# Attention and experts in one kernel: the first maxima in two-bank tiles, and the row maxima of later pairs one slot later

## The chip, the cores and the metric

One core of a Trainium2 chip runs the program once. The metric is the device time of that execution in microseconds, the median of several runs. TensorE (PE) has a granted clock that the profile shows; its two levels are 1.2 and 2.4 GHz, and 1.00 is the upper one.

## The reference

Attention over 8 batches of 8 heads, 1152 keys of 64 numbers, queries pooled by two (576), followed by a layer of 8 experts, of which each token uses one.

```python
    q_pool = q.reshape(B, H, S // factor, factor, D).mean(axis=3)
    scores = scale * np.matmul(q_pool, k.transpose(0, 1, 3, 2))
    scores = scores - np.max(scores, axis=-1, keepdims=True)
    attn = np.exp(scores)
    attn = attn / (np.sum(attn, axis=-1, keepdims=True) + 1e-09)
    return np.matmul(attn, v).astype(np.float32)
    ...
        h = np.maximum(x[mask] @ w1[e], 0.0)
        out[mask] = gate_w[mask, None] * (h @ w2[e])
```

## The kernel before

Two heads make a pair; 32 pairs, counted from 0, go through attention one behind the other, and 18 blocks of tokens go through the experts behind them. Numbers of 32 bits are split into a high and a low half of 16 bits (`hi`/`lo`, `qh`, `VH`/`vl`, `Pe`/`Pl`), so that TensorE works on 16-bit operands.

A pair takes three passes. The **maximum pass** (`maxpass`, L952) multiplies rounded queries `QB` with rounded keys `hi`, in tiles of 512 keys, for nine groups of 128 queries (L964), and VectorE reduces each tile to one maximum per query (`mp`, L965). The last 128 keys of four groups share one tile (L972, L973), and the last group has one of its own. At the end VectorE reduces the maxima of all tiles to `m` (L925), TensorE transposes `m` into a row (L929), VectorE scales it (`mr`, L938), and a DMA on SP's queue puts the row below the queries in `B2` (L939), where the score matmuls subtract it. The **scores** (L1031, L1032) are computed in tiles of 432 columns, ScalarE takes the exponential (`Pe`, L1033), and ScalarE and VectorE make its low half (`Pl`, L1014, L1016). The **products** with the values (L1090 to L1092) add up in `xp`, which VectorE scales (L1108 to L1113) and splits (`x`, L1059).

The order of all engines is written out by the program itself: `attention` counts steps, 18 to a pair, and a string of letters per step says when the score generator (`s`), the product generator (`v`) and the maximum generator (`M`, and at some steps `X`) advance by one tile. Tables such as `T_MAX` say at which step, counted from the pair's own first score, the maximum pass of a pair joins the queue; `T_MX2` and `T_MX3` do so for pairs 2 and 3. When a pass has advanced past its last tile, `m` is issued at once and the transpose at the end of that step. The queues of the engines are in order: what stands behind a waiting instruction waits too.

The start differs. The first pair's queries and keys come in pieces (`load_kq`). VectorE adds the two halves of the pooled queries (L1189), ScalarE copies them into `QB` (L1191, L1194) and rounds the keys to `hi` (`split_hi`, L794), GpSimd makes the low halves (`split_lo`, L810). `first_max` (L981) computes the maxima of the first five groups in 15 tiles of 384 keys, one PSUM bank and one reduction each (L988), with a dummy matmul (`busy`) behind every tile, which keeps TensorE's clock up. Then follow the row of these five groups, `T_PRE` tiles of the rest of the pass with two dummies before each, and the first step. SP's queue meanwhile issues the placements of `hi`, `qh` and `lo` into the score operands `B1` and `B2`, for the first head and a part of the second, and then the row. GpSimd fills the last row of both `B2` with a constant (L1180). `alone` marks a VectorE instruction that uses the port of SBUF which it shares with GpSimd, `behind` lets a GpSimd instruction wait for the last one so marked.

Of the kernel before, what the change touches and what calls it, by code (L numbers as in the profile page):

```python
# [9 lines left out]
F32 = mybir.dt.float32  # L10
# [6 lines left out]
ALU = mybir.AluOpType  # L17
AX = mybir.AxisListType
PSUM = bass.MemoryType.PSUM
# [3 lines left out]
P = 128  # L23
# [5 lines left out]
S = 1152  # L29
D = 64  # L30
# [7 lines left out]
ROW = 16.0  # L38
# [29 lines left out]
T_QH = (-26, -32)  # L68
T_HI = (-29, -24)
T_LO = ((-26, -26, -23), (-23, -26, -23))  # L70
T_MAX = -24
T_PLACE = -17
T_REST = -13
ST = 2
# [68 lines left out]
DONE = object()  # L143
ORD = ('NvJMvsvMsvXF', 'JvvsMvvXFvv', 'vFvvsJvXv')
FIRST = (0, 1)
T_PRE = 3
TWO_ROWS = (1,)
X_ALL = 8
X_SOME = 105
X_IN = 3  # L150
T_MX2 = -23
T_MX3 = -23
FIN = 0
FD = 0
PD = 0
# [8 lines left out]
def drain(g):  # L164
    for _ in g:
        pass
# [528 lines left out]
def attention(tc, ctx, att, ident, npairs, xpool, on_two, on_split, on_scale, jobs, side, set_pm, started, ahead, hip, own_port):  # L695
# [3 lines left out]
    nc = tc.nc  # L699
# [2 lines left out]
    const = ctx.enter_context(tc.tile_pool(name="acon", bufs=1))  # L702
    pvl = ctx.enter_context(tc.tile_pool(name="avl", bufs=3))
    sm = ctx.enter_context(tc.tile_pool(name="asm", bufs=3))
    ps_max = ctx.enter_context(tc.tile_pool(name="psmax", bufs=3, space=PSUM))
    ps_sc = ctx.enter_context(tc.tile_pool(name="pssc", bufs=3, space=PSUM))
    ps_pv = ctx.enter_context(tc.tile_pool(name="pspv", bufs=2, space=PSUM))
    small = lambda: ps_pv.tile([P, 512], F32, name="pj", tag="pv")
    some = lambda i: ps_max.tile([P, 512], F32, name="pm") if i in IN_PM else small()
    set_pm(some)  # L710
# [2 lines left out]
    B2, QB, VH, VS = [], [], [], []  # L713
# [8 lines left out]
    st = {p: {} for p in range(npairs)}  # L722
    made = set()
# [59 lines left out]
    def place_qb(p):  # L783
        qh = st[p]["qh"]
        for j in range(2):
            r = slice(j * D, (j + 1) * D)
            move(QB[p % 2].rearrange("p u n -> p (u n)")[r, j * SQ:(j + 1) * SQ], qh[r])

    def split_hi(p, i):
        s = st[p]  # L790
        made.add((p, f"hi{i}"))
        n = 2 if p > 1 else 3
        r = slice(i * S // n, (i + 1) * S // n)
        nc.scalar.copy(s["hi"][:, r], s["k"][:, r])  # L794

    def split_lo(p, i):

        s = st[p]
        made.add((p, f"lo{i}"))
        if p > 1:  # L800
            need(p, ("qh", "hi0", "hi1")[i])
        n = 1 if p > 1 else 3
        if i < n:
            r = slice(i * SQ // n, (i + 1) * SQ // n)
            o, t, h = s["lo"][:, S:KQ], s["q"], s["qh"]
        else:
            w = 576 if n == 1 else 288
            r = slice((i - n) * w, (i - n + 1) * w)
            o, t, h = s["lo"], s["k"], s["hi"]
        x = nc.gpsimd.tensor_tensor(o[:, r], t[:, r], h[:, r], op=ALU.subtract)  # L810
        if p > 2:
            behind(x)

    kcol = lambda j: slice(j * S, (j + 1) * S)
# [18 lines left out]
    def place_q(p, heads):  # L833

        s = st[p]
        for b in (B2[p % 2], s["B1"]):
            for j in heads:
                move(b[0:D, qcol(j)], s["qh"][half[j]])
# [8 lines left out]
    def place_lo(p, heads, k):  # L847

        s = st[p]
        for j in heads:  # L850
            if k:
                move(B2[p % 2][0:D, kcol(j)], s["lo"][half[j], 0:S])
            else:
                move(s["B1"][D:P, qcol(j)], s["lo"][half[j], S:KQ])
# [126 lines left out]
    def first_max(p):  # L981

        s = st[p]
        mp = s["mp"] = sm.tile([P, 9, 3], F32, name="mp")
        for i, (u, t) in enumerate([(u, t) for us, ts in (((0, 1), (0, 1)), ((2, 3), (0, 1)), (range(4), (2,)), ((4,), range(3))) for t in ts for u in us]):
            pt = ps_sc.tile([P, 512], F32, name="psc") if i % 2 else ps_max.tile([P, 512], F32, name="pm")
            nc.tensor.matmul(pt[:, 0:384], QB[p % 2][:, u], s["hi"][:, t * 384:(t + 1) * 384], start=True, stop=True)
            nc.vector.tensor_reduce(mp[:, u, t:t + 1], pt[:, 0:384], op=ALU.max, axis=AX.X)  # L988
            busy(1, 256)
            yield  # L990
        busy(4)
        row(p, mp, 0, 5)()
# [179 lines left out]
    def busy(n, w=512):  # L1172
        for _ in range(n):
            nc.tensor.matmul(idle[:, 0:w], zero[:, 0:P], zero[:, 0:w], start=True, stop=True, skip_group_check=True)

    busy(7)
    for i in range(2):
        nc.vector.memset(QB[i], 0.0)
    for i in range(2):
        nc.gpsimd.memset(B2[i][D:D + 1, 0:2 * S], ROW)  # L1180
    split_q(0)
    q0, qb = st[0]["q"][:, 0:SQ], QB[0].rearrange("p u n -> p (u n)")
    if npairs > 1:
# [2 lines left out]
    for n, i in ((0, 0), (2, 1), (2, 2)):  # L1186
        if i < 2:
            both = st[0]["q"].rearrange("p (w n) -> p w n", w=2)
            nc.vector.tensor_tensor(both[:, 0, half_q(i)], both[:, 0, half_q(i)], both[:, 1, half_q(i)], op=ALU.add)  # L1189
        if i == 0:  # L1190
            nc.scalar.copy(qb[0:D, half_q(0)], q0[0:D, half_q(0)])  # L1191
        split_hi(0, i)
        if i == 1:
            nc.scalar.copy(qb[0:D, half_q(1)], q0[0:D, half_q(1)])  # L1194
        for _ in range(2):
            next(first)
    nc.scalar.copy(st[0]["qh"], q0)
    nc.scalar.copy(qb[D:P, SQ:S], q0[D:P])
    for i in (3, 4, 5, 6, 0, 1, 2):
# [3 lines left out]
    place_q(0, (0,))  # L1203
    place_lo(0, (0,), 1)
    place_lo(0, (0,), 0)
    place_q(0, (1,))
    place_lo(0, (1,), 0)
    if npairs > 1:
        split_q(1)
        for i in range(3):  # L1210
# [10 lines left out]
        for i in (3, 4, 5, 6):  # L1221
            split_lo(1, i)
    drain(first)
    mp0 = st[0]["mp"]
    if npairs > 1:
        place_qb(1)
    place_lo(0, (1,), 1)
    place_k(0, (1,))
    power(0)
# [548 lines left out]
```

## Time and profile before

| what | value |
|---|---|
| median of 3 runs | 1113.68 us (1113.42 to 1114.29) |
| the profiled execution | 1112.91 us |
| its span | 1110.9 us |
| busy: PE, DVE, ACT, POOL | 1096.5, 956.1, 897.0, 428.6 us |
| first scores of pair 0 | 16.66 us after the span's start |

The span runs from the first to the last instruction of the profiled execution. Engines: PE is TensorE (PEld its weight loads), DVE VectorE, ACT ScalarE, POOL GpSimd, SP SyncE, which here issues DMAs. A matmul's line lasts from its start to its modelled end and overlaps with the next, so the distance between starts is what a matmul costs. A bracket behind a line gives the idle time of that engine before it and what ended it.

### The profile page before, as it was taken

What the parts mean: (1) busy time and instruction counts of PE and PEld (TensorE: products, weight loads), DVE (VectorE), ACT (ScalarE), POOL (GpSimd) and SP (SyncE); (2) the same over time, 40 slices, a digit from 0 to 9 for tenths busy, and PEclk for the clock granted to TensorE, in tenths of its full rate; (3) what the DMA queues carried; (4) which work ended last, traced back from release to release, by engine and by line L of the source; (5) the groups of instructions that cost most, each with busy time, mean ns of one, the idle gap of its engine ahead of it and who ended that gap; (6) DMA issues with size and microseconds to landing.
All of it is one profiled execution on the core that took longest, in us unless ns stands there. A gap on an engine that the chain in (4) does not pass through costs nothing. (4 is left out here: it accounts for less than half of the span.)

```text
span 1110.9 us, 36821 instructions
## 1 busy us (share of the span) xinstructions
PE 1096.5 (99%) x15104; PEld 811.7 (73%) x15104; DVE 956.1 (86%) x1960; ACT 897.0 (81%) x1444; POOL 428.6 (39%) x426
## 2 busy tenths in 40 slices
PE   7999999999999999999999999999999999999997
PEld 4777777777777777777777777876677677667675
DVE  8999999999999999999999999789987666756751
ACT  6899999999999999999999999876556566656651
POOL 9765434454444354444534453132122231121111
PEclk9999999999999999999999999999999999999999
DMA  8758756758676667576676755699889999999980
GB/s 253 185 166 200 182 156 177 196 152 198 157 201 175 168 184 191 143 185 180 181 179 165 205 132 127 178 294 312 278 258 239 301 307 290 271 275 287 271 194 33
DMA packets 173248, 228.46 MB, mean 206 GB/s; under 512 B 91039, under 2 KB 125503, under 8 KB 173072
## 3 DMA queue, kind: packets, MB, share of 16 engines
q1 hardware_dynamic: 166944, 206.25, 68.0%
q0 software_dynamic: 6128, 19.79, 6.5%
q8 instruction: 120, 1.97, 0.7%
q14 instruction: 56, 0.46, 0.2%
HBM read 141.92 MB, written 18.99 MB: 145 GB/s over the span
## 5 line engine op out<-in xcount | busy, mean ns | idle before, releaser
L1033 ACT ACTIVATE Pe<-psc 128x432 int32<-128x432 f32 x768 | 375.5, 526 | 35.6 <-PE psc L1032 27.1
L965 DVE TENSOR_REDUCE mp<-pm 128x1 f32<-128x512 f32 x566 | 372.9, 684 | 11.7 <-PE pm L964 4.4
L1090 PE MATMUL xp<-VH,Pe 128*128 128x65 f16 x2880 | 372.8, 193 | 0.0
L1092 PE MATMUL xp<-VS,Pl 128*128 128x65 f16 x2880 | 372.1, 193 | 0.0
L1091 PE MATMUL xp<-vl,Pe 128*128 128x64 f16 x2880 | 370.9, 192 | 0.0
L1091 PEld LDWEIGHTS <-Pe 128*128 128x128 f16 x2880 | 267.6, 98 | 88.0
L1031 PE MATMUL psc<-B 128*128 128x432 f16 (+2 forms) x1152 | 304.1, 286 | 0.9 <-ACT Pe L1033 0.9
L1032 PE MATMUL psc<-B 65*128 65x432 f16 (+2 forms) x1152 | 304.8, 287 | 0.0
L1090 PEld LDWEIGHTS <-Pe 128*128 128x128 f16 x2880 | 271.9, 98 | 39.8 <-issue 1.7
L1092 PEld LDWEIGHTS <-Pl 128*128 128x128 f16 x2880 | 266.5, 97 | 0.0
L1014 ACT ACTIVATE Pl<-Pe 128x1152 f16<-128x1152 uint16 x186 | 216.5, 1164 | 5.9
L964 PE MATMUL pm<-hi,QB 128*128 128x512 f16 x566 | 213.8, 379 | 1.1 <-DVE mp L965 1.0
L1459 PE MATMUL ph<-xpart,w1l 128*128 128x256 f16 x544 | 148.3, 273 | 0.0
L1458 PE MATMUL ph<-xpart,w1h 128*128 128x256 f16 x544 | 148.3, 273 | 0.0
L1457 PE MATMUL ph<-xpart,w1h 128*128 128x256 f16 x544 | 148.3, 273 | 0.0
L810 POOL TENSOR_TENSOR lo<-rawk,hi 128x576 f16<-128x576 f32 (+1 forms) x68 | 83.3, 1228 | 152.8 <-DVE Pl L1016 131.4
L908 POOL TENSOR_SCALAR VH<-rawv,sc 128x512 f16<-128x512 f32 (+1 forms) x63 | 108.5, 1723 | 76.4 <-PE xp L1092 34.5
L1032 PEld LDWEIGHTS <-B 65*128 65x128 f16 x1152 | 112.9, 98 | 24.1 <-issue 1.1
L1031 PEld LDWEIGHTS <-B 128*128 128x128 f16 x1152 | 112.5, 98 | 5.6 <-issue 0.3
L1548 PE MATMUL po<-w2h,hl 128*128 128x512 f16 x288 | 109.1, 379 | 0.0
L1547 PE MATMUL po<-w2l,hh 128*128 128x512 f16 x288 | 109.1, 379 | 0.0
L1546 PE MATMUL po<-w2h,hh 128*128 128x512 f16 x288 | 109.1, 379 | 0.0
(304 smaller groups left out, 1767.9 us busy)
## 6 DMA issues: line engine op xcount, KB each, us to landing
w2r<-in_w_dram SPq DMA_DIRECT2D x72, 512.0 KB
w1r<-in_w_dram SPq DMA_DIRECT2D x68, 512.0 KB
rawv<-in_att_dram SPq DMA_DIRECT2D x32, 576.0 KB
B<-hi SPq DMA_DIRECT2D x128, 144.0 KB
rawq<-in_att_dram SPq DMA_DIRECT2D x31, 576.0 KB
rawk<-in_att_dram SPq DMA_DIRECT2D x31, 576.0 KB
B<-qh SPq DMA_DIRECT2D x128, 72.0 KB
B<-lo SPq DMA_DIRECT2D x64, 144.0 KB
```

Of the source, the lines that this page charges most:

```text
L964: nc.tensor.matmul(pm, QB[p % 2][:, u], s["hi"][:, t * 512:(t + 1) * 512], start=True, stop=True)
L965: nc.vector.tensor_reduce(mp[:, u, t:t + 1], pm, op=ALU.max, axis=AX.X)
L1014: nc.scalar.activation(low, rest, AF.Copy, scale=LOW)
L1031: nc.tensor.matmul(o, b1[:, ks], b1[:, qs], start=True, stop=False, skip_group_check=True)
L1032: nc.tensor.matmul(o, b2[:, ks], b2[:, qs], start=False, stop=True, skip_group_check=True)
L1033: nc.scalar.activation(Pe[:, D + x0:D + x1], pt, AF.Exp, scale=1.0 / 16)
L1090: nc.tensor.matmul(out, Ph[:, qs], vh[:, c, j, 0:D + 1], start=c == 0 and g == 0, stop=False, skip_group_check=True)
L1091: nc.tensor.matmul(out[:, 0:D], Ph[:, qs], vl[:, c, j], start=False, stop=False, skip_group_check=True)
L1092: nc.tensor.matmul(out, Pl[:, qs], vs[:, c, j, 0:D + 1], start=False, stop=c == NKC - 1, skip_group_check=True)
L1457: nc.tensor.matmul(o, hi[:, c, fs], xh[:, :, c], start=c == 0, stop=False)
L1458: nc.tensor.matmul(o, hi[:, c, fs], xl[:, :, c], start=False, stop=False)
L1459: nc.tensor.matmul(o, lo[:, c, fs], xh[:, :, c], start=False, stop=c == 3)
```

## The change

`first_max` takes tiles of two banks: two maxima tiles of 384 keys are computed into one PSUM tile and reduced by one instruction, eight reductions in place of 15. The pool of these tiles is closed before the pools of the maximum and score tiles are opened. VectorE instead of ScalarE rounds the first third of the keys, and VectorE instead of GpSimd fills the second `B2`. The first additions are marked `alone`, and GpSimd's second low part of the keys waits for them. Three placements of the second head (two of `qh`, one of `lo`) are issued behind the first row and behind pair 1's `QB`. `T_PRE` becomes 4. The maximum passes of pair 3 and of pairs 4 to 31 join the queue one step later (`T_MX3`, `T_MAX`).

```diff
--- before.py
+++ after.py
@@ -68,7 +68,7 @@
 T_QH = (-26, -32)
 T_HI = (-29, -24)
 T_LO = ((-26, -26, -23), (-23, -26, -23))
-T_MAX = -24
+T_MAX = -23
 T_PLACE = -17
 T_REST = -13
 ST = 2
@@ -143,13 +143,13 @@
 DONE = object()
 ORD = ('NvJMvsvMsvXF', 'JvvsMvvXFvv', 'vFvvsJvXv')
 FIRST = (0, 1)
-T_PRE = 3
+T_PRE = 4
 TWO_ROWS = (1,)
 X_ALL = 8
 X_SOME = 105
 X_IN = 3
 T_MX2 = -23
-T_MX3 = -23
+T_MX3 = -22
 FIN = 0
 FD = 0
 PD = 0
@@ -702,9 +702,10 @@
     const = ctx.enter_context(tc.tile_pool(name="acon", bufs=1))
     pvl = ctx.enter_context(tc.tile_pool(name="avl", bufs=3))
     sm = ctx.enter_context(tc.tile_pool(name="asm", bufs=3))
-    ps_max = ctx.enter_context(tc.tile_pool(name="psmax", bufs=3, space=PSUM))
-    ps_sc = ctx.enter_context(tc.tile_pool(name="pssc", bufs=3, space=PSUM))
     ps_pv = ctx.enter_context(tc.tile_pool(name="pspv", bufs=2, space=PSUM))
+    two_banks = ExitStack()
+    ps_two = two_banks.enter_context(tc.tile_pool(name="pstwo", bufs=3, space=PSUM))
+    ps_max = ps_sc = None
     small = lambda: ps_pv.tile([P, 512], F32, name="pj", tag="pv")
     some = lambda i: ps_max.tile([P, 512], F32, name="pm") if i in IN_PM else small()
     set_pm(some)
@@ -808,7 +809,7 @@
             r = slice((i - n) * w, (i - n + 1) * w)
             o, t, h = s["lo"], s["k"], s["hi"]
         x = nc.gpsimd.tensor_tensor(o[:, r], t[:, r], h[:, r], op=ALU.subtract)
-        if p > 2:
+        if p > 2 or (p, i) == (0, 4):
             behind(x)
 
     kcol = lambda j: slice(j * S, (j + 1) * S)
@@ -982,11 +983,17 @@
 
         s = st[p]
         mp = s["mp"] = sm.tile([P, 9, 3], F32, name="mp")
-        for i, (u, t) in enumerate([(u, t) for us, ts in (((0, 1), (0, 1)), ((2, 3), (0, 1)), (range(4), (2,)), ((4,), range(3))) for t in ts for u in us]):
-            pt = ps_sc.tile([P, 512], F32, name="psc") if i % 2 else ps_max.tile([P, 512], F32, name="pm")
-            nc.tensor.matmul(pt[:, 0:384], QB[p % 2][:, u], s["hi"][:, t * 384:(t + 1) * 384], start=True, stop=True)
-            nc.vector.tensor_reduce(mp[:, u, t:t + 1], pt[:, 0:384], op=ALU.max, axis=AX.X)
+        def bank(pt, i, u, t):
+            nc.tensor.matmul(pt[:, i], QB[p % 2][:, u], s["hi"][:, t * 384:(t + 1) * 384], start=True, stop=True)
             busy(1, 256)
+
+        for us, ts in ((0, 1), (0,)), ((0, 1), (1,)), ((2, 3), (0,)), ((2, 3), (1,)), ((0, 1), (2,)), ((2, 3), (2,)), ((4,), (0, 1)), ((4,), (2,)):
+            pt = ps_two.tile([P, 2, 512], F32, name="two")[:, :, 0:384]
+            for i, (u, t) in enumerate([(u, t) for u in us for t in ts]):
+                bank(pt, i, u, t)
+            n, o = len(us) * len(ts), mp[:, us[0]:us[-1] + 1, ts[0]:ts[-1] + 1]
+            o = o[:, :, 0] if len(ts) == 1 else o[:, 0]
+            nc.vector.tensor_reduce(o, pt[:, 0:n], op=ALU.max, axis=AX.X)
             yield
         busy(4)
         row(p, mp, 0, 5)()
@@ -1176,8 +1183,8 @@
     busy(7)
     for i in range(2):
         nc.vector.memset(QB[i], 0.0)
-    for i in range(2):
-        nc.gpsimd.memset(B2[i][D:D + 1, 0:2 * S], ROW)
+    nc.vector.memset(B2[1][D:D + 1, 0:2 * S], ROW)
+    nc.gpsimd.memset(B2[0][D:D + 1, 0:2 * S], ROW)
     split_q(0)
     q0, qb = st[0]["q"][:, 0:SQ], QB[0].rearrange("p u n -> p (u n)")
     if npairs > 1:
@@ -1186,14 +1193,17 @@
     for n, i in ((0, 0), (2, 1), (2, 2)):
         if i < 2:
             both = st[0]["q"].rearrange("p (w n) -> p w n", w=2)
-            nc.vector.tensor_tensor(both[:, 0, half_q(i)], both[:, 0, half_q(i)], both[:, 1, half_q(i)], op=ALU.add)
+            alone(nc.vector.tensor_tensor(both[:, 0, half_q(i)], both[:, 0, half_q(i)], both[:, 1, half_q(i)], op=ALU.add))
         if i == 0:
             nc.scalar.copy(qb[0:D, half_q(0)], q0[0:D, half_q(0)])
-        split_hi(0, i)
+        if i:
+            split_hi(0, i)
+        else:
+            made.add((0, "hi0"))
+            nc.vector.tensor_copy(st[0]["hi"][:, 0:384], st[0]["k"][:, 0:384])
         if i == 1:
             nc.scalar.copy(qb[0:D, half_q(1)], q0[0:D, half_q(1)])
-        for _ in range(2):
-            next(first)
+        next(first)
     nc.scalar.copy(st[0]["qh"], q0)
     nc.scalar.copy(qb[D:P, SQ:S], q0[D:P])
     for i in (3, 4, 5, 6, 0, 1, 2):
@@ -1203,8 +1213,6 @@
     place_q(0, (0,))
     place_lo(0, (0,), 1)
     place_lo(0, (0,), 0)
-    place_q(0, (1,))
-    place_lo(0, (1,), 0)
     if npairs > 1:
         split_q(1)
         for i in range(3):
@@ -1221,9 +1229,14 @@
         for i in (3, 4, 5, 6):
             split_lo(1, i)
     drain(first)
+    two_banks.close()
+    ps_max = ctx.enter_context(tc.tile_pool(name="psmax", bufs=3, space=PSUM))
+    ps_sc = ctx.enter_context(tc.tile_pool(name="pssc", bufs=3, space=PSUM))
     mp0 = st[0]["mp"]
     if npairs > 1:
         place_qb(1)
+    place_q(0, (1,))
+    place_lo(0, (1,), 0)
     place_lo(0, (1,), 1)
     place_k(0, (1,))
     power(0)
```

On VectorE at the very start, before the change:

```order
L1178 MEMSET QB_112 128x576
L1178 MEMSET QB_114 128x576
L1189 TENSOR_TENSOR rawq<-rawq 128x288
L988 TENSOR_REDUCE mp<-pm 128x1
L988 TENSOR_REDUCE mp<-psc 128x1
L1189 TENSOR_TENSOR rawq<-rawq 128x288
L988 TENSOR_REDUCE mp<-pm 128x1
L988 TENSOR_REDUCE mp<-psc 128x1
```

and now:

```order
L1185 MEMSET QB_109 128x576
L1185 MEMSET QB_111 128x576
L1186 MEMSET B_1_110 1x2304
L1196 TENSOR_TENSOR rawq<-rawq 128x288
L1203 CAST hi<-rawk 128x384
L996 TENSOR_REDUCE mp<-two 128x2
L1196 TENSOR_TENSOR rawq<-rawq 128x288
L996 TENSOR_REDUCE mp<-two 128x2 x6
L996 TENSOR_REDUCE mp<-two 128x1
L926 TENSOR_REDUCE m_271<-mp 128x5
```

The fill of `B2` and the rounding have come in, ahead of the first addition and behind it, and the reductions take two tiles each.

On VectorE at the end of the maximum pass of pair 10, an even pair, before the change:

```order
L965 TENSOR_REDUCE mp<-pm 128x1 x2
L314 TENSOR_REDUCE wide_5054<-lg 128x72
L973 TENSOR_REDUCE mp<-pm 128x1
L925 TENSOR_REDUCE m_5783<-mp 128x9
L1059 SCALAR_TENSOR_TENSOR x_5706<-x_5257,sc,x_5705 128x9x64
L1016 TENSOR_SCALAR Pl_118<-Pe_117 128x576
L938 TENSOR_SCALAR mr<-pm 9x128
L965 TENSOR_REDUCE mp<-pm 128x1
```

and now:

```order
L966 TENSOR_REDUCE mp<-pm 128x1
L314 TENSOR_REDUCE wide_5043<-lg 128x72
L966 TENSOR_REDUCE mp<-pm 128x1
L974 TENSOR_REDUCE mp<-pm 128x1
L1066 SCALAR_TENSOR_TENSOR x_5692<-x_5245,sc,x_5691 128x9x64
L1023 TENSOR_SCALAR Pl_115<-Pe_114 128x576
L926 TENSOR_REDUCE m_5800<-mp 128x9
L1115 TENSOR_SCALAR rs<-xp 128x5
```

The reduction to `m` has moved behind the split `x` and the low half `Pl`. On TensorE 29 matmuls stand between the last maximum's matmul and the transpose of `m` in this pair, 15 before.

On TensorE at the same place of pair 11, an odd pair (each matmul has its weight load, LDWEIGHTS, ahead), the last matmul of the maximum pass (`pm`) and what follows it, before the change:

```order
L972 MATMUL pm<-hi,QB_114 128x128
...
L1031 MATMUL psc<-B_5431 128x432
...
L1031 MATMUL psc<-B_5431 128x144
...
L1031 MATMUL psc<-B_5431 128x288
...
L929 MATMUL pm<-ident,m_6336 9x128
```

and now:

```order
L1038 MATMUL psc<-B_5420 128x432
...
L973 MATMUL pm<-hi,QB_111 128x128
...
L1038 MATMUL psc<-B_5420 128x144
...
L1038 MATMUL psc<-B_5420 128x288
...
L930 MATMUL pm<-ident,m_6337 9x128
```

The last maximum's matmul has moved behind the scores of 432 columns: 7 matmuls stand between it and the transpose, 15 before. On VectorE `m` still follows it at once in this pair.

## Rows read from the trace of the kernel before

**Rows 1.** The page's busy line, then busy time by stretch, 200 to 400 us.

```profile
PE 1096.5 (99%) x15104; PEld 811.7 (73%) x15104; DVE 956.1 (86%) x1960; ACT 897.0 (81%) x1444; POOL 428.6 (39%) x426
...
200.00:400.00 200.00, 199.99 (x3468) 155.16 (x3466) 191.72 (x425) 190.23 (x327) 89.31 (x77) 1.00 0.69 179
```

**Rows 2.** Timeline of PE around the transpose of pair 7's row (start us, us, engine, ...).

```profile
166.30 0.38 PE L964 MATMUL pm<-hi,QB 128*128 128x512 f16 x1
...
167.12 0.23 PE L1031 MATMUL psc<-B 128*128 128x144 f16 x1
...
167.50 0.19 PE L1090 MATMUL xp<-VH,Pe 128*128 128x65 f16 x1
...
167.56 0.19 PE L1092 MATMUL xp<-VS,Pl 128*128 128x65 f16 x1
167.89 0.28 PE L929 MATMUL pm<-ident,m 128*9 128x128 f32 x1
```

**Rows 3.** Timeline of DVE over the same stretch.

```profile
166.72 0.69 DVE L965 TENSOR_REDUCE mp<-pm 128x1 f32<-128x512 f32 x1 [0.15 <-PE pm L964]
167.33 0.29 DVE L973 TENSOR_REDUCE mp<-pm 128x1 f32<-128x128 f32 x1
167.65 0.18 DVE L925 TENSOR_REDUCE m<-mp 128x9 f32<-128x27 f32 x1
167.75 0.81 DVE L1059 SCALAR_TENSOR_TENSOR x<-x,sc,x 128x576 f16<-128x576 f32 x1
168.47 0.46 DVE L1016 TENSOR_SCALAR Pl<-Pe 128x576 f16<-128x576 uint16 x1
168.84 0.27 DVE L938 TENSOR_SCALAR mr<-pm 9x128 f16<-9x128 f32 x1
```

**Rows 4.** Timeline of DVE and PE around the transpose of pair 9's row.

```profile
211.04 0.18 DVE L925 TENSOR_REDUCE m<-mp 128x9 f32<-128x27 f32 x1
...
211.14 0.97 DVE L1059 SCALAR_TENSOR_TENSOR x<-x,sc,x 128x576 f16<-128x576 f32 x1
...
211.53 0.27 PE L929 MATMUL pm<-ident,m 128*9 128x128 f32 x1
...
212.03 0.45 DVE L1016 TENSOR_SCALAR Pl<-Pe 128x576 f16<-128x576 uint16 x1
```

**Rows 5.** Timeline of PE while pairs 8 and 26 are scored: scores that wait for ACT.

```profile
215.29 0.19 PE L1092 MATMUL xp<-VS,Pl 128*128 128x65 f16 x1
215.45 0.28 PE L1031 MATMUL psc<-B 128*128 128x288 f16 x1
...
610.60 0.19 PE L1092 MATMUL xp<-VS,Pl 128*128 128x65 f16 x1
610.76 0.28 PE L1031 MATMUL psc<-B 128*128 128x288 f16 x1
```

**Rows 6.** Timeline of DVE, the start.

```profile
1.27 1.14 DVE L1178 MEMSET QB<- 128x576 uint32 x2
3.81 0.46 DVE L1189 TENSOR_TENSOR rawq<-rawq 128x288 f32<-128x288 f32 x1 [1.40 <-DMA rawq<-in_att_dram]
...
6.74 0.75 DVE L1189 TENSOR_TENSOR rawq<-rawq 128x288 f32<-128x288 f32 x1 [0.16 <-DMA rawq<-in_att_dram]
7.42 0.55 DVE L988 TENSOR_REDUCE mp<-pm 128x1 f32<-128x384 f32 x1
...
13.62 0.17 DVE L925 TENSOR_REDUCE m<-mp 128x5 f32<-128x15 f32 x1
```

**Rows 7.** Timeline of POOL and PE, the start.

```profile
1.14 2.01 POOL L1180 MEMSET B<- 1x2304 f16 x1
...
13.94 0.27 PE L929 MATMUL pj<-ident,m 128*5 128x128 f32 x1 [1.79 <-DVE m L925]
...
16.66 0.35 PE L1031 MATMUL psc<-B 128*128 128x432 f16 x1
```

**Rows 8.** Waits of PE, 0 to 60 us: total, times, longest.

```profile
PE pm L964 <- DVE mp L965: 1.0, 3, 0.5
```

## The prediction

> **What bounds the kernel now.** I read the page's busy line first, then the busy time by stretch, then the timeline engine by engine around the places that the change moves. The page says TensorE 99% [rows 1], which alone proves little, as the ends of matmuls are modelled. But from 200 to 400 us TensorE has 199.99 of 200 us, VectorE 191.72, ScalarE 190.23, GpSimd 89.31, at the full granted clock of 1.00 (2.4 GHz) [rows 1]. In the steady part TensorE never stops, the next two engines are close behind, and all work in front of a TensorE instruction that is late is paid in full. The chain of waits reaches back only over the last stores and says nothing here. So I ask two questions: when does the steady part begin, and where will TensorE wait that it doesn't now?
>
> A wait of TensorE shows between starts, not as idle time. In pair 7 the last product before the row's transpose starts at 167.56, the two products from 167.50 on took 0.03 each, and the transpose starts at 167.89 [rows 2]: it could have started at 167.59 and waited 0.30 us. VectorE says for what [rows 3]: the 512-column maximum starts at 166.72 (0.42 after its matmul's 166.30; its line shows 0.15 of waiting for TensorE, so VectorE had nothing queued), the 128-column one at 167.33, the reduction of the nine maxima `m` at 167.65; the transpose follows 0.24 after that. Matmul to transpose takes 0.42 + 0.61 + 0.32 + 0.24 = 1.59 on VectorE, and TensorE has 167.59 - 166.30 = 1.29 of other work. Pair 9 has the usual order: `m` starts at 211.04 and the transpose at 211.53, 0.49 later instead of 0.24 [rows 4], so there VectorE is ahead and TensorE doesn't wait.
>
> **The change part by part.** *Maxima one slot later* (`T_MAX`, `T_MX3`). No instruction is added, but the two orders that I showed ahead change for every pair from 8 on. Before, all of them have 15 matmuls between the last maximum's matmul and the row's transpose. Now the odd pairs 9 to 31 (12) have 7, and the even pairs 8 to 30 (12) have 29.
>
> Odd pairs: the new order on TensorE and VectorE is, instruction for instruction from that 512-column matmul to the transpose, the one pair 7 had before. So the price is a row of this trace: 0.30 us [rows 2, 3]. 12 x 0.30 = 3.6 us. VectorE can't be further ahead than in pair 7, where it waited for TensorE; it can be further behind, so this is a lower bound.
>
> Even pairs: 29 matmuls look safe, but `m` now stands behind the split `x` and the low half `Pl` on VectorE. From the 512-column matmul: 0.42 + 0.61 as above; the 128-column maximum until the next instruction, at most 0.32 and, as `x` doesn't need its result, I take 0.25; `x` 0.72 in pair 7 (167.75 to 168.47 [rows 3]) or 0.89 in pair 9 (211.14 to 212.03 [rows 4]); `Pl` 0.37 (168.47 to 168.84 [rows 3]); `m` to transpose 0.24. Sum 2.61, with the slower `x` and the full 0.32 2.85. TensorE's work: the 1.29 of pair 7, six more products (0.18), four score matmuls (0.38, as 167.12 to 167.50 [rows 2]) and twelve products (0.36): 2.21. It waits 0.40 to 0.64. I take 0.40, since pair 7's `x` is the unhindered one: 12 x 0.40 = 4.8 us.
>
> Given back: pair 7 itself loses its short order (22 matmuls now), -0.3. In every other pair TensorE now waits for ScalarE's exponential, first at 215.29 to 215.45, last at 610.60 to 610.76, ten times [rows 5]; without the 0.03 of the product itself that is 0.13 each. It comes 4 us behind an odd pair's transpose, and none follows pair 7's. TensorE waiting there lets ScalarE catch up, so these 1.3 us go. For other small waits of this kind I put 0.6, an estimate between nothing and another 1.3. The row itself comes up to about 1 us later in the even pairs; its first use is the first score of the pair, more than two steps behind, so I let nothing wait for it.
>
> Net of the steady part: 3.6 + 4.8 - 0.3 - 1.3 - 0.6 = +6.2 us.
>
> *The start.* Fifteen reductions become eight. The 13 behind the second addition of queries take from 7.42 to 13.62 [rows 6], 0.47 each; a 512-column one takes 0.61 [rows 3], so 128 columns cost 0.14, 384 cost 0.42 and the fixed part is 0.05: joining six pairs saves 0.3. The second addition takes 0.75 beside GpSimd, the first 0.46 alone [rows 6]; with `alone`/`behind` GpSimd's split waits: -0.3. Against this, a joined reduction starts only when both its matmuls are done, 0.27 later (the matmul and the dummy between), and VectorE now clears the second `B2`. VectorE's two clears of 576 take 1.14 together and end at 2.41 [rows 6], 1.0 ns an element; by that 2304 elements take 2.3 us, by GpSimd's row for the same clear 2.01 [rows 7]. I take 2.0: it ends at 4.4, not before 3.81 where the first addition starts [rows 6], so the first maxima come 0.6 later. The rounding by VectorE next to the copy by ScalarE returns some 0.4 of it, and the second addition, which waits for its DMA at 6.74 anyway [rows 6], hides the rest but some 0.15. Sum at `m`: -0.3 - 0.3 + 0.27 + 0.15, so 0.2 earlier; 0.35 if the clear were hidden. The Trainium skill ("VectorE: DVE Perf Modes", section "Zero memsets can be issued as uint32 (trn2)") says that a memset takes one cycle per element whatever the type, 0.96 GHz by its table, and only zeros are issued as 32-bit words: 2.4 us for these 2304 halves, an estimate from that page. By it the row comes 0.2 later instead of earlier, and the sum is 0.4 us higher.
>
> `T_PRE` 4 puts two dummies and one maximum more ahead of the first scores. Between transpose (13.94) and first scores (16.66) TensorE works without a gap [rows 7], so they start later, by about 0.65 less the 0.2; the maximum (0.22) is only moved, and the waits behind it, above all the 1.0 us for VectorE's maxima [rows 8], take up the two dummies. VectorE's earlier start counts: -0.2, between -0.35 (the clear hidden) and +0.45 (0.65 less 0.2, nothing taken up).
>
> The second head's three placements go behind the row and `QB` on SP's queue. They are used nine steps later; this cover is about 11 us for some 2 us of issuing: nothing. The clear leaves GpSimd idle until it has rounded keys: nothing.
>
> **Sum:** +6.2 - 0.2 = +6.0 on the profiled execution's 1112.91 (span 1110.9): 1118.9. The median of the runs stands 0.77 above that execution, so 1119.7. A measurement of this kernel can tell about 0.2% (2.2 us) from no change.
>
> **The rivals.** *Hidden behind ScalarE (not slower):* ScalarE is 95% busy and already holds TensorE every other pair [rows 1, 5]. If the pair's length were set by ScalarE, a wait at the transpose would only replace a later one. It decides the sign if it gives back over 6 us, that is 0.25 in each of 24 pairs; the trace shows 0.13 in every other pair, and TensorE lacks 0.01 us of 200. What is left would be the start: 1113.5. *The change doesn't do what the order says at the chip*, and what is given back (0.3 + 1.3 + 0.6) and the start's 0.35 are all that is left: 1111.1. It needs both the odd and the even wait to be missing. *VectorE falls behind:* at 96% it may not have pair 7's idle 0.15 in every pair, and `x` is the slow one beside GpSimd: 12 x 0.45 + 12 x 0.64, with pair 7's 0.3, 1.3 of ScalarE's waits and the start's 0.2 off: 1125.0.
>
> **How the numbers follow.** Forecast 0.70, VectorE behind 0.08, hidden behind ScalarE 0.18, gain 0.04. The forecast's own range is 1118.8 (another 0.7 given back, the start at -0.35) to 1123.0 (even pairs at 0.57 with the slower `x`, 1.3 given back, the start at +0.45). The range of 8 in 10 goes down to the hidden case, 1113.2, and up to 1123.0. Slower by over 0.2% (above 1115.9) takes the forecast and VectorE behind: 0.78; within 0.2% 0.18; faster 0.04.
>
> **What would show it.** Right: between starts TensorE has 0.3 us ahead of the odd pairs' transposes and 0.4 or more ahead of the even ones, 24 times from pair 8 on; the gaps of 0.13 are gone; the part behind attention is as long as before; `m` of the first row starts within 0.4 us of 13.4. The memset's row shows 2.0 or 2.4. Wrong: transposes that follow their predecessors at 0.03 us, or a pair's length of before in spite of such waits.

## The result, and the profile after

The changed kernel takes 1124.3 us (median), before 1113.86: ratio 1.0089 (95% interval 1.0078 to 1.0101), 9.9 us slower. Forecast were 1119.7 and a range up to 1123.0. The sign and the mechanism of the steady part held; the time lies 1.3 us above the range, above all because the forecast had nothing for the step from attention to the experts (1.9 us in the trace).

The profile that came with this comparison is of one disturbed execution of 6446 us, so the rows of "after" below are of the same kernel run once more (run e1_after_again: 1124.04 us profiled, span 1122.1). The page's busy line and the busy time by stretch, 200 to 400 us:

```profile
PE 1100.4 (98%) x15106; PEld 812.4 (72%) x15106; DVE 955.8 (85%) x1955; ACT 898.9 (80%) x1443; POOL 423.8 (38%) x425
...
200.00:400.00 200.00, 198.46 (x3435) 153.53 (x3432) 189.02 (x423) 189.52 (x324) 87.37 (x76) 1.00 0.66 174
```

Against [rows 1] TensorE lacks 1.54 us in this stretch where it lacked 0.01. The clock is 1.00 as before.

Where the 11.2 us between the two spans (1110.9 and 1122.1) lie is read from the starts of four instructions of TensorE. Timeline of PE before: first scores of pairs 8 and 30, last product of attention, first product of the experts:

```profile
196.10 0.35 PE L1031 MATMUL psc<-B 128*128 128x432 f16 x1
...
679.68 0.35 PE L1031 MATMUL psc<-B 128*128 128x432 f16 x1
...
720.81 0.19 PE L1092 MATMUL xp<-VS,Pl 128*128 128x65 f16 x1
720.84 0.28 PE L1457 MATMUL ph<-xfirst,w1h 128*128 128x256 f16 x1
```

The same four after:

```profile
198.76 0.35 PE L1038 MATMUL psc<-B 128*128 128x432 f16 x1
...
688.01 0.35 PE L1038 MATMUL psc<-B 128*128 128x432 f16 x1
...
730.28 0.19 PE L1099 MATMUL xp<-VS,Pl 128*128 128x65 f16 x1
732.18 0.28 PE L1470 MATMUL ph<-xfirst,w1h 128*128 128x256 f16 x1 [1.70 <-DVE x L1120]
```

| stretch | before | after | more |
|---|---|---|---|
| to the first scores of pair 8 | 196.10 | 198.76 | 2.66 |
| pairs 8 to 29 | 483.58 | 489.25 | 5.67 |
| pair 30 to the last product | 41.13 | 42.27 | 1.14 |
| last product to the experts' first | 0.03 | 1.90 | 1.87 |
| the rest | 390.06 | 389.92 | -0.14 |

Three places are longer: the start, the steady part, and one that the forecast didn't have, the step from attention to the experts. Two things must be kept in mind with the table: the transpose of pair 8's row lies ahead of its first scores, so its wait is in the first line, and one 512-column maximum (0.22 us) has moved from the first line's stretch into the third's.

The steady part first. Timeline of PE after, at the row transposes of pairs 7, 8 and 9, each behind the product that starts before it (compare [rows 2]):

```profile
170.41 0.19 PE L1099 MATMUL xp<-VS,Pl 128*128 128x65 f16 x1
171.33 0.28 PE L930 MATMUL pm<-ident,m 128*9 128x128 f32 x1 [0.72 <-DVE m L926]
...
193.34 0.19 PE L1099 MATMUL xp<-VS,Pl 128*128 128x65 f16 x1
193.72 0.28 PE L930 MATMUL pm<-ident,m 128*9 128x128 f32 x1 [0.18 <-DVE m L926]
...
214.37 0.19 PE L1099 MATMUL xp<-VS,Pl 128*128 128x65 f16 x1
214.69 0.28 PE L930 MATMUL pm<-ident,m 128*9 128x128 f32 x1
```

From start to start less the 0.03 of a product: 0.89, 0.35, 0.29. All 24 transposes from pair 8 on wait like this: the twelve odd ones 0.29 to 0.64 (4.3 us in sum, eight of them 0.29 or 0.30), the twelve even ones 0.34 to 0.51 (4.5 in sum). The view of waits, which counts idle time by modelled ends only and so less, puts it first; before, it had no line for these transposes:

```profile
PE pm L930 <- DVE m L926: 4.5, 17, 0.7
PE ph L1470 <- DVE x L1120: 1.7, 1, 1.7
```

Timeline of DVE after, ahead of pair 8's transpose: `m` stands behind `x` and `Pl`, as the forecast's order said.

```profile
192.19 0.28 DVE L974 TENSOR_REDUCE mp<-pm 128x1 f32<-128x128 f32 x1
192.40 0.81 DVE L1066 SCALAR_TENSOR_TENSOR x<-x,sc,x 128x576 f16<-128x576 f32 x1
193.12 0.45 DVE L1023 TENSOR_SCALAR Pl<-Pe 128x576 f16<-128x576 uint16 x1
193.49 0.18 DVE L926 TENSOR_REDUCE m<-mp 128x9 f32<-128x27 f32 x1
```

The waits for ScalarE [rows 5] are gone, all ten.

### The profile page after: what moved, and what is told of

The parts are those of the page before. It is cut to its first block, busy times and chain, and to the rows that moved or that the text cites. A ratio compares the mean times of both kernels' runs of the same rounds, so it can differ in the third digit from the quotient of the medians.

```text
span 6444.4 us, 36818 instructions
## 1 busy us (share of the span) xinstructions
PE 6435.7 (100%) x15106; PEld 3380.3 (52%) x15106; DVE 1006.7 (16%) x1955; ACT 960.7 (15%) x1443; POOL 410.8 (6%) x425
## 5 line engine op out<-in xcount | busy, mean ns | idle before, releaser
L1097 PE MATMUL xp<-VH,Pe 128*128 128x65 f16 x2880 | 1411.8, 502 | 0.0
L1099 PE MATMUL xp<-VS,Pl 128*128 128x65 f16 x2880 | 1307.7, 465 | 0.0
L1039 PE MATMUL psc<-B 65*128 65x432 f16 (+2 forms) x1152 | 1293.2, 1129 | 0.0
L1098 PE MATMUL xp<-vl,Pe 128*128 128x64 f16 x2880 | 1291.9, 458 | 0.0
L1038 PE MATMUL psc<-B 128*128 128x432 f16 (+2 forms) x1152 | 1243.3, 1088 | 0.0
L1098 PEld LDWEIGHTS <-Pe 128*128 128x128 f16 x2880 | 798.8, 277 | 810.7 <-issue 804.8
L1097 PEld LDWEIGHTS <-Pe 128*128 128x128 f16 x2880 | 732.2, 254 | 393.1 <-issue 380.2
L965 PE MATMUL pm<-hi,QB 128*128 128x512 f16 x566 | 931.3, 1649 | 0.0
L1099 PEld LDWEIGHTS <-Pl 128*128 128x128 f16 x2880 | 668.9, 232 | 0.0
L1471 PE MATMUL ph<-xpart,w1h 128*128 128x256 f16 x544 | 568.9, 1046 | 0.0
L1472 PE MATMUL ph<-xpart,w1l 128*128 128x256 f16 x544 | 568.9, 1046 | 0.0
L1470 PE MATMUL ph<-xpart,w1h 128*128 128x256 f16 x544 | 567.7, 1044 | 0.0
```

The lines of the kernel that those rows point to most:

```text
L965: nc.tensor.matmul(pm, QB[p % 2][:, u], s["hi"][:, t * 512:(t + 1) * 512], start=True, stop=True)
L1038: nc.tensor.matmul(o, b1[:, ks], b1[:, qs], start=True, stop=False, skip_group_check=True)
L1039: nc.tensor.matmul(o, b2[:, ks], b2[:, qs], start=False, stop=True, skip_group_check=True)
L1097: nc.tensor.matmul(out, Ph[:, qs], vh[:, c, j, 0:D + 1], start=c == 0 and g == 0, stop=False, skip_group_check=True)
L1098: nc.tensor.matmul(out[:, 0:D], Ph[:, qs], vl[:, c, j], start=False, stop=False, skip_group_check=True)
L1099: nc.tensor.matmul(out, Pl[:, qs], vs[:, c, j, 0:D + 1], start=False, stop=c == NKC - 1, skip_group_check=True)
```

## The experiments

Differences to the kernel before are in us, from the ratio of runs on the same chip, with the 95% interval in brackets.

**The parts apart.** Four kernels on one chip: the changed kernel again; with the old slots; the new slots alone; the old slots and 3 maxima ahead.

```diff
e2_old_slots, on the changed kernel
-T_MAX = -23
+T_MAX = -24
-T_MX3 = -22
+T_MX3 = -23
e3_slots_alone, on the kernel before: the opposite
e4_pre3, on e2
-T_PRE = 4
+T_PRE = 3
```

> The changed kernel once more, for a trace of an undisturbed execution. Every theory: about 1124.3 us, 10 to 11 above before. Theory A (the rows' transposes of the steady part cost it all): TensorE stands 0.3 us ahead of the transposes of odd pairs and 0.4 to 0.8 ahead of those of even pairs, 24 times from pair 8 on, 9 to 12 us in sum; the first row's m within 0.4 us of 13.4. Theory B (the start costs part): first scores of pair 0 2 us or more later than before's 16.66, and a steady part that is only some 6 us longer. Theory C (VectorE's backlog): the transposes' waits sum to 6 to 8 us, and 3 us or more appear at matmuls that wait for score banks or first maxima.

> The changed kernel with the slots of the maxima as before, so that only the start differs from before. Theory A: 1113.3 to 1114.3, the same as before within 0.5 us, no gap ahead of the transposes of pairs 8 to 31. Theory B: 1116 or more, 2 to 4 us above before. Theory C: as A.

> The kernel before with the slots of the maxima as changed, so that only the steady part differs. Theory A: 9.5 to 11 us above before (1123.4 to 1124.9). Theory B: 6 to 8 us above before (1120 to 1122). Theory C: as A, with the gaps spread over transposes and other matmuls.

> As the run with the old slots, and with one maximum fewer ahead of the first scores (3, as before). Theory A: within 0.4 us of the run with the old slots. Theory B, if the later first scores are what the start costs: 0.6 us or more faster than that run.

Measured: changed +9.5 [7.9, 11.0], old slots +3.1 [2.1, 4.1], slots alone +5.1 [3.6, 6.7], old slots with 3 ahead +3.2 [2.0, 4.6]. Theory A falls: the slots carry 5.1 by themselves and 6.4 as the difference to e2, out of 9.5, the rest of the change about 3 us. B is right that there is a second cost, but not with its reason: one maximum fewer ahead (e4) changes nothing. C falls too, the gaps stand at the transposes.

Where the 3 us of the old slots are, their longest wait behind the start tells first. View of waits of PE, old slots:

```profile
PE ph L1470 <- DVE x L1120: 1.7, 1, 1.7
```

The experts' first product `ph` waits for `x`, which reads the last pair's outputs and has nothing to do with the experts. The two share only a PSUM bank: the changed kernel opens the pool of the output banks ahead of the two others, so the outputs lie where the experts' first tiles are placed.

**The banks.** The kernel before once more, the old slots with the router's two banks taken first, and the kernel before with nothing changed but the order of its pools.

```diff
e6_router_banks, on e2
+    ps_r = ctx.enter_context(tc.tile_pool(name="psr", bufs=PR, space=PSUM, reuse_waits="tile"))
     ps_x = ctx.enter_context(tc.tile_pool(name="psx", bufs=3 - PR, space=PSUM, reuse_waits="tile"))
...
-    ps_r = ctx.enter_context(tc.tile_pool(name="psr", bufs=PR, space=PSUM, reuse_waits="tile"))
e7_pv_first, on the kernel before
+    ps_pv = ctx.enter_context(tc.tile_pool(name="pspv", bufs=2, space=PSUM))
     ps_max = ctx.enter_context(tc.tile_pool(name="psmax", bufs=3, space=PSUM))
     ps_sc = ctx.enter_context(tc.tile_pool(name="pssc", bufs=3, space=PSUM))
-    ps_pv = ctx.enter_context(tc.tile_pool(name="pspv", bufs=2, space=PSUM))
```

> The kernel before once more, for a trace from the chip of the other runs and as a null comparison. Every theory: ratio 1.000 within 0.001. The four runs so far have a gap of about 0.7 us between products of the last pair that no semaphore explains, and the first trace of the kernel before has none. If that gap belongs to the chip or to where the code lies, it is or is not here too: here too means that 0.7 us of the difference between the first two traces is no effect of the change.

> The changed start with the old slots, and with the router's two PSUM banks taken ahead of the experts', so that the experts' first products no longer get a bank that the last pair's outputs still hold. Theory D (the new order of the PSUM pools makes the experts wait for the last pair's outputs): TensorE goes from the last pair's products to the experts' first without a gap (1.7 us before), and the run is 1.7 to 1.9 us below the run with the old slots, 1116.8 on that chip, 1.5 above before. Theory B (all of it from the start): as the run with the old slots, within 0.4 us.

> The kernel before with the pool of the two output banks opened ahead of the two others and nothing else: no instruction moves. Theory D: 1.7 to 1.9 us above before, with a gap of 1.7 us ahead of the experts' first product. Theory B: the same as before within 0.3 us.

Measured: before again +0.3 [-0.7, 1.3], router's banks +1.8 [0.8, 2.8], output pool first +2.4 [1.4, 3.5]. Timeline of PE of the last one, in which no instruction moves against before:

```profile
721.65 0.19 PE L1092 MATMUL xp<-VS,Pl 128*128 128x65 f16 x1
723.47 0.28 PE L1457 MATMUL ph<-xfirst,w1h 128*128 128x256 f16 x1 [1.62 <-DVE x L1113]
```

The wait is there (1.79 beyond the product's 0.03), and with the router's banks first it is gone (last product 723.61, experts' first 723.64). Theory D holds: 1.8 us come from the order in which pools are opened. One gap of 0.7 ahead of scores of the last pair, which e1 to e4 have (idle 0.5, ended by "issue"), is in none of these three traces. In all the runs told of here it came in every one of the ten on three of the chips, whatever the kernel, and in none of the eight on the two others, so 0.7 of the 1.14 in the table's third line is no effect of the change.

**The start, engine by engine.** The clear of `B2` was put back on GpSimd (e8), then late on GpSimd (e9), then with 3 maxima ahead (e10), then the joined maxima by themselves (e11).

```diff
e8_memset_back, on e6 (old slots, router's banks first)
-    nc.vector.memset(B2[1][D:D + 1, 0:2 * S], ROW)
-    nc.gpsimd.memset(B2[0][D:D + 1, 0:2 * S], ROW)
+    for i in range(2):
+        nc.gpsimd.memset(B2[i][D:D + 1, 0:2 * S], ROW)
e9_late_clear, on e6
-    nc.vector.memset(B2[1][D:D + 1, 0:2 * S], ROW)
...
         for i in (3, 4, 5, 6):
             split_lo(1, i)
+        nc.gpsimd.memset(B2[1][D:D + 1, 0:2 * S], ROW)
e10_late_clear_pre3, on e9: T_PRE = 3
e11_joined_alone, on e8: T_PRE = 3, and
-            nc.vector.tensor_copy(st[0]["hi"][:, 0:384], st[0]["k"][:, 0:384])
+            split_hi(0, i)
```

> The run with the router's banks first, and both clears of B2 on GpSimd as before. If the clear on VectorE is what delays the start (the memset row of 1.98 us, which begins 0.5 us after the clears ahead of it end): the first addition starts at 3.8 (4.94 with the clear), m of the first row at 13.6 to 13.9 (14.74), and the run is 0.8 to 1.1 us below the run with the router's banks first, within 0.7 us of before. Rival (the start's length is set by the queries' second half and by the maxima, whichever engine clears): m at 14.4 or later and no more than 0.3 us.

> The run with the router's banks first (old slots, the changed start, rounding by VectorE), with the second B2 cleared by GpSimd behind the second pair's first splits, where neither engine's start waits for it. Theory E (either place of the clear delays the start by 1.1: on VectorE it holds the first addition, on GpSimd it holds VectorE's rounding, 1.60 long instead of 0.35): first addition at 3.8, rounding 0.35 long, second addition at 6.8, m of the first row at 13.5 to 13.9, and the run 0.8 to 1.1 below the run with the router's banks first, 0.8 to 1.1 above before. Rival F (the joined maxima and the second half of the queries set the start's length): m at 14.4 or later and no gain over 0.3.

> The same with 3 maxima ahead of the first scores instead of 4. Theory E with the full price of the fourth (one maximum and two dummies, 0.65): first scores at 16.6 to 16.9, and the run 0.4 to 0.7 below the run with the late clear, within 0.5 of before. Rival: the same as the run with the late clear, since the two dummies only fill time in which TensorE waits for VectorE.

> The joined maxima by themselves: old slots, the router's banks first, both clears on GpSimd, rounding by ScalarE, 3 maxima ahead. By the forecast's sum for joining (0.3 and 0.3 less 0.27) m would be 0.3 earlier than before's 13.62, 13.3. By the changed kernel's trace joining saves nothing (the six last take 4.9 instead of 5.6, but VectorE stands 0.65 for the first of them, and the second addition waits behind the first joined maximum): m at 13.7 to 14.1. The run within 0.6 of before either way.

Measured: +1.2 [0.2, 2.2], +1.5 [0.4, 2.5], +1.8 [0.8, 2.8], +1.6 [0.6, 2.6], none told from the +1.8 of e6. So theory E fails as an account of time. Its picture of the engines was right in part: timeline of DVE, the changed kernel's start, then e8's and e9's rounding:

```profile
2.93 1.98 DVE L1186 MEMSET B<- 1x2304 f16 x1 [0.52 <-issue]
4.94 0.46 DVE L1196 TENSOR_TENSOR rawq<-rawq 128x288 f32<-128x288 f32 x1
5.32 0.35 DVE L1203 CAST hi<-rawk 128x384 f16<-128x384 f32 x1
...
7.87 0.45 DVE L1196 TENSOR_TENSOR rawq<-rawq 128x288 f32<-128x288 f32 x1
...
14.74 0.17 DVE L926 TENSOR_REDUCE m<-mp 128x5 f32<-128x15 f32 x1
```

```profile
4.21 1.60 DVE L1203 CAST hi<-rawk 128x384 f16<-128x384 f32 x1
```

```profile
4.17 0.36 DVE L1202 CAST hi<-rawk 128x384 f16<-128x384 f32 x1
```

The clear does hold the first addition (it starts at 4.94, before at 3.81 [rows 6]), and on GpSimd (3.58 to 5.59 in e8) it holds VectorE's rounding until it ends. Yet when `m` came at 13.46 (e10) nothing was won, because TensorE then stood up to 24.86 for values (`VS`) that GpSimd's late clear had delayed: an experiment that moved its cost instead of removing it.

**Each part of the start alone.** On the kernel before, but for f3, which is e11 with the placements where they were.

```diff
f1_pre4_alone
-T_PRE = 3
+T_PRE = 4
f2_placements_alone (f3: the opposite, on e11)
     place_lo(0, (0,), 0)
-    place_q(0, (1,))
-    place_lo(0, (1,), 0)
     if npairs > 1:
         split_q(1)
...
         place_qb(1)
+    place_q(0, (1,))
+    place_lo(0, (1,), 0)
     place_lo(0, (1,), 1)
f4_vector_start: the clear of B2[1] and the rounding of the first keys on VectorE, as in the change
```

> The kernel before with 4 maxima ahead of the first scores. If the fourth with its two dummies is a price of its own: first scores 0.65 later, 0.5 to 0.7 above before. If the dummies only fill waits: within 0.2 of before.

> The kernel before with the second head's placements behind the first row and QB. If SyncE's queue is what sets the second pair's start: QB of pair 2 lands 0.5 to 1.5 later and TensorE waits that long for it at 38 to 40 (0.14 in before), 0.5 to 1.5 above before. By the forecast (covered by nine steps): within 0.2 of before.

> The joined maxima, with the second head's placements ahead of the row as before (rounding, clears and 3 maxima as before, router's banks first). If the joined maxima cost: m 0.4 to 0.8 later than before's 13.62 and 0.4 to 0.8 above before. If the placements cost in the run of the joined maxima alone (1.74 of waiting at 38 to 40): that wait is below 0.5 here.

> The kernel before with one clear of B2 and the first rounding on VectorE, nothing else. If the clear holds the first addition: addition at 4.9 instead of 3.8, m 0.5 to 1.1 later, 0.5 to 1.1 above before. By the forecast (0.6 later less 0.4 of rounding, hidden by the second addition's DMA): within 0.2 of before.

Measured: fourth maximum -0.3 [-1.3, 0.7], placements +1.2 [0.2, 2.2], joined maxima with old placements -0.1 [-1.1, 0.9], rounding and clear on VectorE -0.3 [-1.3, 0.7]. Only the placements show. Timeline of SP with the placements moved (f2), from the low half on:

```profile
11.46 1.18 SPq L736 DMA_DIRECT2D B<-lo  x2
15.63 0.84 SPq L939 DMA_DIRECT2D B<-mr  x1
...
21.60 0.59 SPq L753 DMA_DIRECT2D rawq<-in_att_dram  x1
...
37.75 1.17 SPq L736 DMA_DIRECT2D QB<-qh  x2
```

The same with the joined maxima and the old placements (f3):

```profile
14.55 0.84 SPq L940 DMA_DIRECT2D B<-mr  x1
...
18.60 0.59 SPq L754 DMA_DIRECT2D rawq<-in_att_dram  x1
...
35.67 1.18 SPq L737 DMA_DIRECT2D QB<-qh  x2
```

And with the old placements and a row as late as f2's (f1):

```profile
15.60 0.84 SPq L939 DMA_DIRECT2D B<-mr  x1
...
19.65 0.59 SPq L753 DMA_DIRECT2D rawq<-in_att_dram  x1
...
34.99 1.17 SPq L736 DMA_DIRECT2D QB<-qh  x2
```

In f2 SP issues nothing from 12.64 to 15.63, when it waits for the row; what it could have issued there comes behind. The next pair's load of queries goes out at 21.60 instead of 18.60, and pair 2's `QB`, last of a long queue, at 37.75 instead of 35.67. Not all of that is the placements': f2's row itself is 1.08 later than f3's, in a start with a slow TensorE (see the last section). Counted from the row, the load goes out 5.97 behind it in f2 and 4.05 in f3 and f1, so 1.9 us are theirs. Timeline of PE, f2, where pair 2's first maximum meets it:

```profile
38.46 0.19 PE L1092 MATMUL xp<-VS,Pl 128*128 128x65 f16 x1
40.16 0.39 PE L964 MATMUL pm<-hi,QB 128*128 128x512 f16 x1 [1.51 <-DMA QB<-qh]
```

In f3 the same two rows are 37.52 and 37.78, and in f1 that maximum doesn't wait. The DMA engines show the hole: the DMA view, 8 to 40 us in slices of 0.8 us, GB/s, f2 and then f3:

```profile
GB/s 426 415 415 297 209 177 215 48 0 0 10 2 98 127 137 100 176 199 213 236 363 430 374 421 427 398 369 323 354 291 170 74 170 35 86 228 228 213 241 128
```

```profile
GB/s 397 398 426 343 238 216 199 74 120 74 38 130 147 202 205 144 357 403 415 392 418 259 300 386 317 297 233 215 161 135 107 144 37 230 230 225 143 74 86 167
```

A wait at this place doesn't tell the two kinds of kernel apart by itself. Between starts it is 1.67 us in f2 and 1.75 in e11, but 0.69 in the changed kernel, and with old placements it is 0.71 in f4 and 0.73 in g1, which are no slower than before. So the placements' price is taken from the runs: f2 against before, and e11 and f3, which differ by the placements alone (+1.6 and -0.1).

**The transpose's wait as a cause.** The changed kernel with the odd pairs' transposes two steps later.

```diff
e12_odd_rows_later
-        later_end(FIN if now[0] > NSTEP else 3 if p == 0 else 2, row(p, mp, u0, 9))
+        later_end((2 if p > 8 and p % 2 else FIN) if now[0] > NSTEP else 3 if p == 0 else 2, row(p, mp, u0, 9))
```

> The changed kernel with the row transposes of odd pairs from 9 on two steps later, so that 46 instead of 7 matmuls stand between the last maximum's matmul and the transpose. Theory A: the twelve gaps of 0.3 to 0.64 ahead of them go (4.2 us in sum), ScalarE's gaps of 0.14 may come back (1.4), and the run is 2.5 to 4.2 below the changed kernel, 5.7 to 7.4 above before. Rival: the gaps are only a cover for a later wait, of the pair's first scores for the row or of VectorE, and the run is as the changed kernel, 9.5 to 10.5 above before.

Measured: +5.5 [3.9, 7.0], 4.0 less than the changed kernel's +9.5. In its trace the odd gaps are gone, the even ones stand, and of ScalarE's waits only 0.3 us in all come back. The 4.3 us of odd gaps return nearly in full. View of waits of PE:

```profile
PE pm L930 <- DVE m L926: 3.3, 13, 0.7
```

**All of it?** The changed kernel with the three parts undone, and with the placements alone undone (edits as above).

> The changed kernel with the three parts undone: old slots, the router's banks first, the second head's placements ahead of the row. Joined maxima, rounding and clear on VectorE and 4 maxima ahead stay. If the three are all: within 0.8 us of before. If the rest costs together: 1 us or more above before. If the rest gains by itself: 0.5 or more below before.

> The changed kernel with the second head's placements ahead of the row as before, nothing else undone. If they cost the 1.2 to 1.7 us found on the other kernels: 8 to 9 above before instead of 9.8 to 10.4, and the wait of pair 2's first maximum at 39 to 40 (0.70) below 0.3. If the loss hangs on the other parts of the start: as the changed kernel.

Measured: +0.3 [-0.7, 1.3] and +9.3 [7.7, 10.8]. With slots, banks and placements undone the kernel is the one before, within what can be measured; joining, rounding, clear and fourth maximum together neither cost nor win. g1 and e6 differ by the placements alone: +0.3 and +1.8. But undoing the placements alone in the changed kernel gave back 0.2, not 1.2 to 1.7, with intervals that allow either. The wait of pair 2's first maximum is gone there, and pair 2's first scores come at 65.37 instead of 66.05. What the placements cost in the changed kernel stays open between 0.2 and 1.7 us. No version beats the kernel before.

## Why the prediction was wrong, point by point

**Odd pairs** (+3.6): right. Gaps of 0.29 or 0.30 in eight of twelve, four larger, +4.3 in sum; the row of pair 7 before was the price. The bound was named as a lower one, and was one.

**Even pairs** (+4.8): right, 4.5 with 0.34 or 0.35 usual. The forecast's chain of `x`, `Pl` and `m` is the one in the trace.

**Pair 7** (-0.3): the sign failed. Its 22 matmuls look safer than the 7 of before, but in the new order `m` stands behind `x` and `Pl` there too, and TensorE waits 0.89 instead of 0.30, so +0.6. The forecast counted matmuls for this pair alone and not VectorE's queue.

**Given back** (-1.3 and -0.6): more. The waits of the steady part before, ten for ScalarE and some for VectorE's maxima and pair 29's row, are nearly all gone (2.6 by the same distances of starts). Net of the steady part by the trace: 4.3 + 4.5 + 0.6 - 2.6 = +6.8. The table gives the same: 0.59 for pair 7, 0.35 for pair 8, 5.67, and 1.14 less the gap of 0.7 and the moved 0.22. Forecast were +6.2; by runs the slots alone are +5.1 [3.6, 6.7].

**The start** (-0.2): failed by the sentence on SP's queue, "this cover is about 11 us for some 2 us of issuing: nothing". It asked when the moved placements are used, not what is queued behind them: the loads of the next pairs and pair 2's `QB`, which go out 1.9 us later behind the row. By runs this costs 1.2 [0.2, 2.2] in f2; in the changed kernel it stays open. The rest of that part's net holds within 1 us: f1, f3 and f4 show nothing.

By the traces the start is 1.9 longer (2.66 less 0.59 of pair 7 and 0.35 of pair 8, with the moved maximum's 0.22 back in). One pair of traces can't price it, though: at pair 8's first scores (196.10 in the first trace) the kernel before, traced again as e5, is 0.49 later, f4 1.11, f1 1.30 and g1 2.02, and by runs none of them differs from before by more than 0.3. The first trace of before, on which the sum stands, was one with a quick start. Timeline of PE, e5 and then g1, first scores of pair 8:

```profile
196.59 0.35 PE L1031 MATMUL psc<-B 128*128 128x432 f16 x1
```

```profile
198.12 0.35 PE L1038 MATMUL psc<-B 128*128 128x432 f16 x1
```

In single terms the start was off: the first `m` was said to come at 13.4 and came at 14.74. The clear began 0.52 later than VectorE was free, the second addition now stands behind a joined maximum (7.87; 6.74 before [rows 6]), and the two joined maxima that VectorE waited for had their matmuls 0.50 and 0.51 apart (0.27 and 0.29 in f3), some 0.45 us in sum (an estimate from these distances). In f3, where no clear is ahead and TensorE ran at its full rate, `m` came at 13.20, 0.42 earlier, close to what the joining's own terms said (-0.3 - 0.3 + 0.27); but in e11, whose compute instructions are the same up to there, it came at 14.34 with TensorE at half the rate, so this agreement is in part luck. The clear's row shows 1.98 us, the forecast's 2.0. By the Trainium skill's rule ("VectorE: DVE Perf Modes", section "Zero memsets can be issued as uint32 (trn2)") it would be 2.4, an estimate; the row differs, and the row decides. The 0.4 between them would not have decided anything, as f4 shows.

**The end** (not in the sum): the step that was missing. The diff shows the pools opened in another order, and the forecast held "the part behind attention is as long as before" as a mark of being right. The experts' first product waits 1.87 us for a bank of the last pair's outputs; without it the time would be about 1122.4, inside the range. By the traces the sum missed 5.2 us (11.2 less 6.0): 1.9 for the bank, 2.1 for the start (1.9, and the 0.2 that it was to win), 0.6 for the steady part, 0.7 for the gap that isn't the change's, less 0.1 for the rest. Against the 9.9 of the runs it missed 3.9: the bank's 1.9, the steady part's 0.6 and f2's 1.2 come to 3.7, but the last of the three isn't shown for the changed kernel.

**The rivals.** "Hidden behind ScalarE" falls: in e12 removing half of the waits returned nearly all of their time, and ScalarE's own waits hardly came back (0.3 us). "VectorE falls behind" falls as well: most odd waits are pair 7's 0.30, not 0.45, and even ones 0.35, not 0.64. Its 1125.0 is close to the time for a reason that isn't there. "The change doesn't do what the order says" falls with the 24 gaps.

## What to carry to other kernels

Moving one group of instructions by a slot is priced by the engine that feeds the next cross-engine step: count what stands ahead on that engine, for every group, the exceptions included. When a transfer is moved behind a wait on an in-order queue, ask what the queue would have sent during the wait, for all that is behind moves by it. And read the order in which pools are opened as part of the schedule: it decides whose bank the next stage inherits, and shows in no list of instructions. What a start costs is read from runs of kernels that differ by one part: two traces of one kernel, before and e5, differ there by 0.5 us.

## What was not expected of the hardware

VectorE's rounding of 384 keys from 32 to 16 bits took 0.35 us, and 1.60 beside GpSimd's clear, ending 0.2 after it. The Trainium skill ("SBUF — State Buffer", section "SBUF: two separate sides") says that the port pair which the two engines share is held by one of them for a whole instruction, and the other is blocked. The row agrees, though GpSimd's clear writes a single partition.

The first 14 us vary with TensorE's rate, in spite of the dummy matmuls. Timeline of PE, first maxima of f2 and then of before, each with a dummy behind it: 0.53 us from one to the next, and 0.28.

```profile
9.02 0.53 PE L987 MATMUL psc<-hi,QB 128*128 128x384 f16 x1
...
9.55 0.53 PE L987 MATMUL pm<-hi,QB 128*128 128x384 f16 x1
```

```profile
8.29 0.33 PE L987 MATMUL psc<-hi,QB 128*128 128x384 f16 x1
...
8.57 0.33 PE L987 MATMUL pm<-hi,QB 128*128 128x384 f16 x1
```

In the first trace of before and in f3 none of the 15 first maxima is slow, in the traces of all other runs told of here 2 to 11 are, six in that of the changed kernel (e1). The granted clock shows it in some of them only: busy time by stretch, PE, f1 and then before, with the granted clock in the third column from the right:

```profile
8.00:12.00 4.00, 3.42 (x15) 0.57 0.99 354
```

```profile
8.00:12.00 4.00, 3.99 (x26) 1.00 0.99 344
```

In f1 the clock was granted at little over the lower of its levels (1.2 of 2.4 GHz) for some 3 us from 8.58 on; in f2 the column stays at 1.00 while the matmuls are as slow. What decides isn't shown: TensorE had stood 0.89 us for the second half of the queries ahead of 8.58 in f1, and as long ahead of 8.01 in before, where the clock stayed at 1.00.

In f1, whose instructions up to the first row are those of before, `m` came 1.04 later (14.66, before 13.62 [rows 6]). Of this 0.57 were there at the first maximum behind the second addition (7.99, before 7.42), as the addition had waited longer for its DMA; the rest came while TensorE was slow. f1's trace is 1.3 us longer than the first one of before, though its runs are not longer than those of before on their chip (-0.3). A first row that is earlier or later by 1 us in one trace proves little about such a kernel's time.
